# Where the narrow matmuls of a software-pipelined attention stand, and four distances of the stages behind it

## The chip, the cores and the metric

The program runs on one core of a Trainium2 chip. The metric is the device time of one execution in microseconds (us). The engines of the core are TensorE (PE, with its weight load PEld), VectorE (DVE), ScalarE (ACT), GpSimd (POOL) and SyncE (SP, which here only issues DMA transfers); each works through its own row of instructions in order and waits on semaphores.

## The reference

Three stages follow each other; the output of one is the input of the next.

```python
# 1: attention inside hash buckets: 2 batches, 8 heads, 768 positions, 64 dims, 6 hash bits
q_bits = (np.einsum('bhsd,dk->bhsk', q, proj) > 0)          # k_bits in the same way
mask = q_bucket[:, :, :, None] == k_bucket[:, :, None, :]
scores = np.where(mask, scale * np.matmul(q, k.transpose(0, 1, 3, 2)), -1000000000.0)
attn = np.exp(scores - np.max(scores, axis=-1, keepdims=True))
attn = attn / (np.sum(attn, axis=-1, keepdims=True) + 1e-09)
attn_out = np.matmul(attn, v)
# 2: mixture of experts on x = attn_out as (1536, 512): 8 experts, top 2, hidden width 1024
noisy_logits = x @ w_gate + np.log1p(np.exp(x @ w_noise)) * noise
out[mask] += top2_w[mask, k, None] * (np.maximum(x[mask] @ w1[e], 0.0) @ w2[e])   # each e, k
# 3: (1536, 512) -> 2048 -> 512
h = x @ w_in
return (h - np.tanh(h)) @ w_out
```

`w_in` and `w_out` come as 64-bit floats and are converted on the chip, in 16 blocks.

## The kernel before

**Attention.** An item is one batch and head; there are 16, and a pair of items (one group) shares the tiles of keys and queries. Time is laid out in *frames*. The table `plan` (filled by `at_frame`, from the offsets in `PLAN`) says which functions run in which frame; item `i` begins at frame 12 `i`. Every frame has one `smax` (a matmul of scores, L414, whose row maximum DVE takes in L415) and one `st_unit` (the transposed scores, two matmuls L448 and L449, then the exponential on ACT, L450). In every second frame comes a `pv` (the product with the values, L474, four matmuls of 64 output columns). Around these stand, once or a few times for each item or group: `prep_t` (three transposes of keys or queries, L271, then copies and remainders on ACT and DVE, L277, L284, L285), `prep_signs` (the hash bits, eight matmuls of 32 columns, L302), `mchain` and `mrows` (the maxima, put as extra rows into the queries, L434 and L438), `vmean` (L462), `psum` (partial sums of the exponentials on POOL or DVE, L483), `sums` (row sums, six matmuls of 32 columns, L490; a copy on ACT, L494, in the next frame; two transposes, L499, in the one after), `evac` (the output copied by ACT, transposed on PE some frames later, L523, scaled by DVE, L527, added up by POOL, L529). Once a pair of heads is done, `gate_t` transposes it for the router (L535) and `gate_wide` multiplies it with the router's weights (32 columns, L596).

**What sets the order.** `frame()` first takes one step of every generator left over from earlier frames and then calls the frame's tasks in the order in which `at_frame` got them. PE, DVE, ACT and SP keep the order in which the code is written; the row of POOL is ordered by the scheduler of the tile framework. Seven PSUM banks go round in rings: three for the tag `a` (turns, signs, sums, output transposes, maxima, router), two for `b` (smax), two for `c` (st_unit); `d`, the outputs, has one. `mchain` takes an `a` bank and keeps it until `mrows` and its DVE product L438 are done.

**The router and the experts.** When batch 0 is through, `gate(0)` runs its chain of small DVE operations in the frames behind `GF` (L624 to L707); its result `sidx` is the index list for `scatter(0)`, twelve indirect DMAs that POOL issues (L711). When batch 1 is through, `gate(1)` runs, and PE fills its steps with pieces of expert 0 (`seg_fine`, taken by `fill`; `FILL` has the number of pieces ahead of each step of the gate; a piece is half of a hidden block, six matmuls L1122, or one output block). Its matmuls for positions are L689 and L755. Segment 1 follows: hidden blocks (L1033 to L1035) and output blocks (L1058 to L1060) in steps numbered `f`; after a few of them all engines take a branch for overflow (L1219, L1220). `load_x(n + 1)` (L1013, L1016) loads the gathered tokens of the next segment and `trans_x` transposes them (L1026; copy on ACT L1027, remainder on DVE L1028). From step `(1, CV1)` on, `convert_more` converts blocks of the 64-bit weights (ACT L877, then DVE) and `fetch64` loads them (L866, L868). `store()` issues finished stores, `fetch()` loads the next expert weights (L840, L842), `next_w()` splits them (ACT L815, POOL L814).

Of the kernel before, what the change touches and what calls it, by code (L numbers as in the profile page):

```python
# [19 lines left out]
WB2 = 2  # L20
PF = 3

FILL = (1, 0, 3, 0, 3, 1, 0, 0, 2, 0, 0, 0)
FILL2 = 2
TX = (2, 2, 0, 0)
BANKS = {'a': [0, 1, 7], 'b': [2, 3], 'c': [4, 5], 'd': [6]}

PLAN = dict(turn=(-23, -15, -19, -10), turn1=(-20, -18, -13, -10), sign=(-12, -7), sign2=5, sign1=(-9, -7), gap=0,
            load=-37, load_v=-13, clear=-8, vsum=-1, vmean=15, gate_t=(58, 55), gate_wide=60, pv=3,
            psum=(5, 7, 8, 11, 14), nmterm=9, evac=13, evac_wait=10, sums=16, sums_wait=0, scatter=19, gate_w=25,  # L30
            pre_w=29, pre_b=-18, zero=26, trans=-12, open=-22, mrows=(13, 13), second=(-3, -2, -1, 0),
            init=(2, 4, 18), gates=(28, 31))

# [13 lines left out]

POOL1 = 7

CV1 = 4  # L50

CVN = 2

# [23 lines left out]
def body(tc, q, k, v, proj, w_gate, w_noise, noise, w1, w2, w_in, w_out, out):  # L77
    nc = tc.nc
    PS = bass.MemoryType.PSUM
    B, H, S, D = q.shape  # L80
# [19 lines left out]
    with ExitStack() as ctx:  # L100
# [792 lines left out]
        def convert_more(n):  # L893

            for _ in range(n):
                if hd.get("cv") is None and RAW64:
                    hd["cv"] = convert(*RAW64.pop(0))
                if hd.get("cv") is not None and next(hd["cv"], 1) is not None:
                    hd["cv"] = None
                    if RAW64:  # L900
                        hd["cv"] = convert(*RAW64.pop(0))
                        next(hd["cv"])
# [4 lines left out]
        def frame(tasks):  # L907

            going = list(running)
            running.clear()  # L910
            for gen in going:
                if next(gen, 1) is None:
                    running.append(gen)
            for f, *a_ in tasks:
                gen = f(*a_)
                if gen is not None and next(gen, 1) is None:
                    running.append(gen)
# [14 lines left out]
        def at_frame(t, f, *a_):  # L932
            plan.setdefault(t, []).append((f, *a_))
# [22 lines left out]
        for g in range(NI // 2):  # L956
            G = 24 * g
            for n, (w_, hf) in enumerate(KQ):
                if g:
                    at_frame(G + PLAN["turn" if g > 1 else "turn1"][n], prep_pool if g == 1 and POOL1 >> n & 1 else prep_t, g, w_, hf)  # L960
                    if w_ == "q":
                        at_frame(G + PLAN["sign" if g > 1 else "sign1"][hf], prep_signs, g, hf)
                else:
                    at_frame(PLAN["second"][n], prep_second, w_, hf)
            at_frame(max(G + PLAN["clear"], 0), clear_m, g)
            at_frame(G + PLAN["vsum"], vsum, g)
            at_frame(G + PLAN["vmean"], vmean, g)
            if g:
                at_frame(max(G + PLAN["load"], 0), load, g)
                at_frame(max(G + PLAN["load_v"], 0), load_v, g)  # L970
            b, P = divmod(g, NP)
            if g + 1 < NI // 2:
                at_frame(G + PLAN["gate_t"][0], gate_t, b, P, 0)
                at_frame(G + PLAN["gate_t"][1], gate_t, b, P, 1)
                if P % 2:
                    at_frame(G + PLAN["gate_wide"], gate_wide, b, (P - 1, P), P == KD4 - 1)
                elif b == B - 1 and P == KD4 - 2:
                    at_frame(G + PLAN["gate_wide"], gate_wide, b, (P,), True)
        GF = 24 * NP + LAG + 28
        at_frame(GF, gate, 0)  # L980
        for wh in range(2):
            at_frame(GF + PLAN["scatter"] + 3 * wh, scatter, 0, wh)
# [35 lines left out]
        def trans_x(n, dc):  # L1018
            e, b, r0, rows, nb = segs[n]
            m, tail = blocks(n)  # L1020
            if dc == 0:
                XH[n] = mx[n % 2].tile([128, KD4, CAP], F32R, name="xh")
                XL[n] = mx[n % 2].tile([128, KD4, CAP], F32R, name="xl")
            ps = bank("a")
            for j, m_ in enumerate([m] * nb + [128] * (tail > 0)):
                nc.tensor.transpose(ps[:, j * m:j * m + m_], xgs[n][0][:m_, j, ck(dc)], ident[:m_, :m_])  # L1026
            nc.scalar.activation(XH[n][:, dc, :rows], ps[:, :rows], AF.Copy)  # L1027
            nc.vector.tensor_tensor(XL[n][:, dc, :rows], ps[:, :rows], XH[n][:, dc, :rows].bitcast(F32), op=ALU.subtract)  # L1028
# [366 lines left out]
        for n in range(1, NSG):  # L1395
            last = n == NSG - 1
            if n == NSG - B:
                rings["C2"] = ctx.enter_context(tc.tile_pool(name="wC2", bufs=WC2, reuse_waits="tile"))
                store()
                mid.close()  # L1400
                del rings["st"]
                rings["C"] = ctx.enter_context(tc.tile_pool(name="wC", bufs=WC, side="right", reuse_waits="tile"))
            if last:
                store()
                m2 = ctx.enter_context(tc.tile_pool(name="m2", bufs=2, side="right", reuse_waits="tile"))
                gb2 = m2.tile([128, 1], F32, name="gb2")
                nc.vector.memset(gb2, G2 / (2 * G3))
                gsb = m2.tile([128, 1], F32, name="gsb")
                nc.vector.memset(gsb, -GS)
            fx = 2 if n == B - 1 else 1  # L1410
            for f in seg_steps(n, None if last else n + 1):
                if (n, f) == (1, IFS):
                    sched.close()
                    overflow()
                    manual()
                store()
                while fn[0] < min(wn[0] + (PF if "st" in rings else 1), len(wsrc)):
                    fetch()
                if not last and f == fx:
                    load_x(n + 1)  # L1420
                for dc in range(0 if last else KD4):
                    if f == (5 + dc // 2 if n == B - 1 else 3 + dc):
                        trans_x(n + 1, dc)
                if (1, CV1) <= (n, f) < (NSG - B, 0):
                    convert_more(CVN)
                    while conv64 and len(RAW64) + (hd.get("cv") is not None) < 2:
                        fetch64(conv64.pop(0))
                if segs[n][1] in (None, B - 1) and (f in LASTW if last else n >= B or f >= W1) or n == NSG - B and f in LASTV:
                    next_w()
                if B <= n < B + WN0 - NF and f == 4:  # L1430
                    next_w()
                for j in range(BC if last else 0):
                    if f == 1 + j // 2:
                        gather(j)
                    if f == 4 + j:
                        combine(j)
                        flush(1)
                    if f == 3 + j:
                        mix(j)
                        flush(1)  # L1440
# [51 lines left out]
```

## Time and profile before

| what | us |
|---|---|
| three timed executions | 941.16, 941.60, 941.63 (median 941.6) |
| the profiled execution's own time | 935.87 |
| span of the profiled execution, first to last instruction | 934.0 |
| PE busy in it | 898.5 (96%) |
| DVE, ACT, POOL busy | 673.6, 540.2, 366.9 |

The span is what the trace covers; the other 1.87 us of the profiled execution lie outside it. The mean clock granted to PE is 0.988 of full speed. Attention ends at about 299 us, expert 0 and the gate of batch 1 at about 334 us, and from about 375 us to the end PE is busy without a gap apart from a few near 660 to 690 us. A matmul's listed length overlaps with that of the next one, so the distance from start to start is its cost on PE.

### The profile page before, as it was taken

What the parts mean: (1) busy time and instruction counts of PE and PEld (TensorE: products, weight loads), DVE (VectorE), ACT (ScalarE), POOL (GpSimd) and SP (SyncE); (2) the same over time, 40 slices, a digit from 0 to 9 for tenths busy, and PEclk for the clock granted to TensorE, in tenths of its full rate; (3) what the DMA queues carried; (4) which work ended last, traced back from release to release, by engine and by line L of the source; (5) the groups of instructions that cost most, each with busy time, mean ns of one, the idle gap of its engine ahead of it and who ended that gap; (6) DMA issues with size and microseconds to landing.
All of it is one profiled execution on the core that took longest, in us unless ns stands there. A gap on an engine that the chain in (4) does not pass through costs nothing.

```text
span 934.0 us, 13624 instructions
## 1 busy us (share of the span) xinstructions
PE 898.5 (96%) x4736; PEld 700.0 (75%) x4736; DVE 673.6 (72%) x1289; ACT 540.2 (58%) x1039; POOL 366.9 (39%) x323
## 2 busy tenths in 40 slices
PE   8999999988899889999999999999999999999998
PEld 3555555544456777888888888888889899989997
DVE  7778777789655617787887878555888677677665
ACT  7658667655356234444444444354777777777765
POOL 6677778763875644000000004502342342342221
PEclk9999999999999998999999999999999999999999
DMA  5635543311401467786959586555420110110000
GB/s 122 176 100 172 168 155 106 114 40 42 156 12 46 168 203 233 274 291 200 314 185 342 188 271 219 169 174 179 134 69 1 57 46 1 57 46 1 35 1 34
DMA packets 104624, 123.72 MB, mean 132 GB/s; under 512 B 32120, under 2 KB 75176, under 8 KB 104552
## 3 DMA queue, kind: packets, MB, share of 16 engines
q1 hardware_dynamic: 100712, 110.23, 37.3%
q0 software_dynamic: 3840, 12.59, 4.0%
q8 instruction: 38, 0.62, 0.3%
q14 instruction: 34, 0.28, 0.1%
HBM read 82.79 MB, written 37.72 MB: 129 GB/s over the span
## 4 chain that ended last, share of the span: by engine, by line
PE 78%; DVE 10%; DMA 4%; POOL 2%; issue 2%; ACT 2%; SPq 1%; DVEq 0%; POOLq 0%; ACTq 0%
PE bank L1034 9%; PE bank L1035 9%; PE bank L1033 9%; PE bank L1060 9%; PE bank L1059 9%; PE bank L1058 8%; PE bank L474 6%; PE bank L448 4%; PE bank L449 3%; PE bank L414 3%; DMA Xg<-x,sidx 3%; PE bank L1075 2%; DVE mx L415 1%; PE bank L1026 1%; PE bank L302 1%
## 5 line engine op out<-in xcount | busy, mean ns | idle before, releaser
L1033 PE MATMUL bank<-xh,wt 128*128 128x384 f32 (+2 forms) x544 | 187.0, 344 | 5.5 <-DVE g_u L1346 2.7
L1034 PE MATMUL bank<-xl,wt 128*128 128x384 f32 (+2 forms) x544 | 183.7, 338 | 0.2 <-DVE xl L1028 0.2
L1035 PE MATMUL bank<-xh,wt 128*128 128x384 f32 (+2 forms) x544 | 183.7, 338 | 0.0
L814 POOL TENSOR_TENSOR wt<-wraw,wt 128x512 fp32r<-128x512 f32 x48 | 68.5, 1449 | 248.2 <-DVE cv_g L879 203.7
L1060 PE MATMUL bank<-wt,hh 128*128 128x512 f32 (+1 forms) x400 | 158.3, 396 | 0.4 <-DVE hh L1051 0.2
L1058 PE MATMUL bank<-wt,hh 128*128 128x512 f32 (+1 forms) x400 | 158.2, 396 | 0.3 <-ACT hh L1049 0.3
L1059 PE MATMUL bank<-wt,hh 128*128 128x512 f32 (+1 forms) x400 | 157.9, 395 | 0.0
L1337 POOL TENSOR_TENSOR g_th<-g_h,g_th 128x384 f32<-128x384 f32 x64 | 67.1, 1049 | 187.9 <-ACT g_th L1336 187.3
L450 ACT ACTIVATE p<-bank 128x384 f32<-128x384 f32 x192 | 92.0, 489 | 69.4 <-PE bank L449 61.3
L415 DVE TENSOR_REDUCE mx<-bank 128x1 f32<-128x384 f32 x192 | 103.1, 551 | 38.4 <-PE bank L414 36.3
L1033 PEld LDWEIGHTS bank<-xh,wt 128*128 128x128 f32 x544 | 103.0, 189 | 15.0 <-DVE g_u L1346 4.8
L1034 PEld LDWEIGHTS bank<-xl,wt 128*128 128x128 f32 x544 | 103.0, 189 | 7.1 <-DVE xl L1028 0.5
L1035 PEld LDWEIGHTS bank<-xh,wt 128*128 128x128 f32 x544 | 102.9, 189 | 3.0
L815 ACT ACTIVATE wt<-wraw 128x1024 fp32r<-128x1024 f32 x80 | 84.2, 1054 | 31.7 <-PE bank L1075 22.4
L1060 PEld LDWEIGHTS bank<-wt,hh 128*128 128x128 f32 (+1 forms) x400 | 74.9, 187 | 18.5 <-DVE hh L1051 0.8
L483 POOL TENSOR_TENSOR ps<-ps,p 128x768 f32<-128x768 f32 x45 | 82.1, 1825 | 10.7 <-ACT p L450 5.9
L1049 ACT ACTIVATE hh<-bank 128x448 fp32r<-128x448 f32 (+1 forms) x80 | 38.0, 475 | 81.0 <-PE bank L1035 40.2
L1058 PEld LDWEIGHTS bank<-wt,hh 128*128 128x128 f32 (+1 forms) x400 | 75.3, 188 | 12.7 <-ACT hh L1049 0.5
L474 PE MATMUL bank<-p,v 128*64 128x384 f32 x384 | 84.7, 520 | 0.0
L1059 PEld LDWEIGHTS bank<-wt,hh 128*128 128x128 f32 (+1 forms) x400 | 75.1, 188 | 12.8
L448 PE MATMUL bank<-qc,kb 108*128 108x384 f32 (+1 forms) x192 | 80.1, 417 | 2.6 <-DVE qc L438 2.5
L1051 DVE SCALAR_TENSOR_TENSOR hh<-bank,hh 128x384 fp32r<-128x384 f32 (+2 forms) x128 | 45.7, 388 | 42.9 <-ACT hh L1049 38.4
(250 smaller groups left out, 1625.5 us busy)
## 6 DMA issues: line engine op xcount, KB each, us to landing
wraw<-in_moe_w_dram SPq DMA_DIRECT2D x128, 256.0 KB
cv_t<-in_moe_w_in_dram SPq DMA_DIRECT2D x16, 512.0 KB
cv_t<-in_moe_w_out_dram SPq DMA_DIRECT2D x16, 512.0 KB
W2f<-cv_w SPq DMA_DIRECT2D x16, 512.0 KB
wraw<-W2f SPq DMA_DIRECT2D x16, 512.0 KB
Xg<-zero SPq DMA_DIRECT2D x14, 512.0 KB
Y<-zero SPq DMA_DIRECT2D x9, 512.0 KB
xy<-Xg SPq DMA_DIRECT2D x6, 768.0 KB
```

The costliest lines, as they stand in the source:

```text
L415: nc.vector.tensor_reduce(MX[i % 2][:, c, hf:hf + 1], ps[:, :HF], op=ALU.max, axis=AX.X)
L448: nc.tensor.matmul(ps[:, :HF], KB[sn(g, par)][r, ck(kc)], QC[sn(g, par)][r, half(hf)], start=True, stop=False)
L450: nc.scalar.activation(hd["p", i, kc][:, half(hf)], ps[:, :HF], AF.Exp, scale=float(D) ** -0.5)
L474: nc.tensor.matmul(hd["o", i][hf * D:(hf + 1) * D, :HF], raw["v", g][:, par, kc], hd["p", i, kc][:, half(hf)], start=(kc == 0), stop=(kc = ...
L483: eng.tensor_tensor(t, hd["p", i, 0] if kc == 1 else t, hd["p", i, kc], op=ALU.add)
L815: nc.scalar.activation(t[:, 0], r, AF.Copy)
L1033: nc.tensor.matmul(ps[:, :n], ws(0, dc), xh[:, dc, :n], start=(dc == 0), stop=False)
L1034: nc.tensor.matmul(ps[:, :n], ws(0, dc), xl[:, dc, :n], start=False, stop=False)
L1035: nc.tensor.matmul(ps[:, :n], ws(1, dc), xh[:, dc, :n], start=False, stop=(dc == KD4 - 1))
L1058: nc.tensor.matmul(ps[:m], a, t[:, 0, 1], start=first, stop=False)
L1059: nc.tensor.matmul(ps[:m], a, t[:, 1, 1], start=False, stop=False)
L1060: nc.tensor.matmul(ps[:m], l, t[:, 0, 1], start=False, stop=last)
```

## The change

It has six parts.

1. `frame()` sorts the frame's tasks: `pv` behind the others, then `sums`, `prep_signs` and `gate_wide`, and `evac` last.
2. Offsets in `PLAN`: `sums` 16 to 17 and `gate_wide` 60 to 64 (the last one, `gate_last`, stays at 60); `turn` and the signs at other frames, so that signs fall into frames that have a `pv`; `vmean` 15 to 17.
3. `evac_wait` 10 to 11: the output's transposes come one frame later behind their copy.
4. `GF` two frames later: `gate(0)` and the two halves of its scatter move with it.
5. `FILL[8]` 2 to 4: two more pieces of expert 0 ahead of gate(1)'s position matmuls.
6. In segment 1: conversion begins at step 7 instead of 4, its first load at step 3; segment 2's tokens are loaded at step 0 instead of 2.

```diff
-FILL = (1, 0, 3, 0, 3, 1, 0, 0, 2, 0, 0, 0)
+FILL = (1, 0, 3, 0, 3, 1, 0, 0, 4, 0, 0, 0)
...
-PLAN = dict(turn=(-23, -15, -19, -10), turn1=(-20, -18, -13, -10), sign=(-12, -7), sign2=5, sign1=(-9, -7), gap=0,
...
+PLAN = dict(turn=(-23, -17, -20, -14), turn1=(-20, -18, -13, -10), sign=(-12, -8), sign2=5, sign1=(-8, -6), gap=0,
...
-CV1 = 4
+CV1 = 3
...
-            for f, *a_ in tasks:
+
+            order = {pv: 1, sums: 2, prep_signs: 2, gate_wide: 2, evac: 3}
+            for f, *a_ in sorted(tasks, key=lambda t_: order.get(t_[0], 0)):
...
-                    at_frame(G + PLAN["gate_wide"], gate_wide, b, (P,), True)
-        GF = 24 * NP + LAG + 28
+                    at_frame(G + PLAN["gate_last"], gate_wide, b, (P,), True)
+        GF = 24 * NP + LAG + 30
...
-            fx = 2 if n == B - 1 else 1
+            fx = 0 if n == B - 1 else 1
...
+                if (1, CV1 + 4) <= (n, f) < (NSG - B, 0):
+                    convert_more(CVN)
                 if (1, CV1) <= (n, f) < (NSG - B, 0):
-                    convert_more(CVN)
```

PE around the sums of item 4 (L490), before. A name left of the arrow is the bank written, `p` and `v` are exponentials and values, `ss` the copied sums.

```order
L474 MATMUL bank_1381<-p,v_98 64x384 x2
L448 MATMUL bank_1389<-qc_168,kb_166 128x384
L449 MATMUL bank_1389<-ql_169,kl_167 128x384
L414 MATMUL bank_1393<-kb_158,qc_160 128x384
L490 MATMUL bank_1396<-ps,ones 32x256 x3
L535 MATMUL bank_1400<-ident,x 128x128 x3
L448 MATMUL bank_1407<-qc_168,kb_166 128x384
L449 MATMUL bank_1407<-ql_169,kl_167 128x384
L414 MATMUL bank_1411<-kb_158,qc_160 128x384
L474 MATMUL bank_1381<-p,v_98 64x384 x2
L499 MATMUL bank_1418<-ident,ss 128x96 x2
```
The same place after:

```order
L535 MATMUL bank_1396<-ident,x 128x128 x3
L271 MATMUL bank_1400<-ident,k 128x128 x3
L448 MATMUL bank_1408<-qc_168,kb_166 128x384
L449 MATMUL bank_1408<-ql_169,kl_167 128x384
L414 MATMUL bank_1412<-kb_158,qc_160 128x384
L474 MATMUL bank_1385<-p,v_98 64x384 x2
L490 MATMUL bank_1419<-ps,ones 32x256 x3
L448 MATMUL bank_1429<-qc_168,kb_166 128x384
L449 MATMUL bank_1429<-ql_169,kl_167 128x384
L414 MATMUL bank_1433<-kb_158,qc_160 128x384
L499 MATMUL bank_1436<-ident,ss 128x96 x2
```
The sums stood alone between wide matmuls and their transposes L499 behind a later value product; now the sums stand directly behind a value product, and L499 three wide matmuls behind them.

PE around the sums of item 12, before; L535 are the transposes for the router that need POOL's L529 of item 11:

```order
L474 MATMUL bank_2979<-p,v_96 64x384 x2
L448 MATMUL bank_2983<-qc_153,kb_151 128x384
L449 MATMUL bank_2983<-ql_154,kl_152 128x384
L414 MATMUL bank_2987<-kb_158,qc_160 128x384
L490 MATMUL bank_2990<-ps,ones 32x256 x3
L535 MATMUL bank_2994<-ident,x 128x128 x3
```
and after:

```order
L474 MATMUL bank_2976<-p,v_96 64x384 x2
L448 MATMUL bank_2983<-qc_153,kb_151 128x384
L449 MATMUL bank_2983<-ql_154,kl_152 128x384
L414 MATMUL bank_2987<-kb_158,qc_160 128x384
L535 MATMUL bank_2990<-ident,x 128x128 x3
L448 MATMUL bank_2995<-qc_153,kb_151 128x384
L449 MATMUL bank_2995<-ql_154,kl_152 128x384
L414 MATMUL bank_2999<-kb_158,qc_160 128x384
L474 MATMUL bank_2976<-p,v_96 64x384 x2
L490 MATMUL bank_3006<-ps,ones 32x256 x3
```
The transposes L535 keep their frame and the sums come one frame behind them, where before they stood ahead.

SP at the load of segment 2's tokens, before, behind the branch:

```order
L842 DMA wraw<-in_moe_w_dram 128x512
L840 DMA wraw<-in_moe_w_dram 128x4x128
L842 DMA wraw<-in_moe_w_dram 128x512
L1013 DMA xy<-Xg 128x1536
L1016 DMA xy<-Xg 128x512
```
and after, ahead of the branch (L1015 and L1018 are L1013 and L1016 of before):

```order
L842 DMA wraw<-in_moe_w_dram 128x512
L1015 DMA xy<-Xg 128x1536
L1018 DMA xy<-Xg 128x512
L840 DMA wraw<-in_moe_w_dram 128x4x128
L842 DMA wraw<-in_moe_w_dram 128x512
L1222 COMPARE_AND_BRANCH
```
The load moved ahead of the branch and of two pairs of weight loads.

## Rows read from the trace of the kernel before

**Rows 1.** Windows: width, PE, PEld, DVE, ACT, POOL busy (instructions), clock, DMA, GB/s.
```profile
75.00:100.00 25.00, 25.00 (x149) 13.96 (x146) 19.79 (x42) 18.00 (x39) 20.34 (x19) 1.00 0.39 118
100.00:125.00 25.00, 23.43 (x142) 13.66 (x140) 18.56 (x40) 18.31 (x38) 19.15 (x17) 1.00 0.45 138
200.00:225.00 25.00, 21.18 (x113) 11.81 (x114) 24.14 (x73) 14.11 (x32) 7.73 (x10) 0.93 0.00 1
375.00:650.00 275.00, 275.00 (x1408) 240.00 (x1408) 203.76 (x292) 123.27 (x176) 30.70 (x22) 1.00 0.71 236
```

**Rows 2.** Waits of PE to 375 us: waiter, releaser: total, times, longest.
```profile
PE bank L414 <- DVE mx L415: 6.2, 5, 1.9
PE bank L523 <- DVE qc L438: 3.1, 2, 1.6
...
PE bank L689 <- DVE M L675: 2.5, 1, 2.5
...
PE bank L1026 <- DMA xy<-Xg: 2.0, 1, 2.0
PE bank L1033 <- ACT xh L1027: 1.5, 1, 1.5
```

**Rows 3.** Timeline of PE: start, length, line, shape, count [idle before <-releaser].
```profile
84.98 0.87 PE L474 MATMUL bank<-p,v 128*64 128x384 f32 x4
85.78 0.52 PE L302 MATMUL bank<-kl,pj 128*32 128x384 f32 x2
...
91.83 0.34 PE L449 MATMUL bank<-ql,kl 128*128 128x384 f32 x1
92.00 0.33 PE L414 MATMUL bank<-kb,qc 128*128 128x384 f32 x1
92.27 0.52 PE L302 MATMUL bank<-kl,pj 128*32 128x384 f32 x2
...
93.05 0.44 PE L448 MATMUL bank<-qc,kb 108*128 108x384 f32 x1
93.33 0.34 PE L449 MATMUL bank<-ql,kl 128*128 128x384 f32 x1
```

**Rows 4.** Timeline of PE around the sums of item 2.
```profile
78.55 0.63 PE L490 MATMUL bank<-ps,ones 128*32 128x256 f32 x6
79.11 0.55 PE L535 MATMUL bank<-ident,x 128*128 128x128 f32 x3
```

**Rows 5.** Timeline of PE, the sums of item 4.
```profile
109.59 0.63 PE L490 MATMUL bank<-ps,ones 128*32 128x256 f32 x6
```

**Rows 6.** Line L494 (ACT): its engine sat idle until.
```profile
  PE bank L490: 6.1, 8
```

**Rows 7.** Timeline of ACT, the same sums of item 2.
```profile
79.90 0.37 ACT L494 ACTIVATE ss<-bank 96x256 f32<-96x256 f32 x1
```

**Rows 8.** Timeline of DVE, the gate of batch 0.
```profile
194.60 1.70 DVE L631 TENSOR_SCALAR g_ln<-g_u 128x48 f32<-128x48 int32 x1
...
226.65 0.17 DVE L707 CAST sidx<-g_p 128x12 int32<-128x12 f32 x1
```

**Rows 9.** Timeline of POOL, first scatter and the step behind it.
```profile
227.13 1.19 POOL L711 DMA_INDIRECT Xg<-x,sidx  x1 [8.12 <-DVE sidx L707]
...
251.19 0.99 POOL L529 TENSOR_TENSOR x<-x,xt 128x384 f32<-128x384 f32 x1
```

**Rows 10.** Timeline of PE, the sums of item 12.
```profile
253.05 1.07 PE L490 MATMUL bank<-ps,ones 128*32 128x256 f32 x6 [2.74 <-DVE ps L483]
```

**Rows 11.** Timeline of PE, two fine pieces of expert 0.
```profile
301.54 0.27 PE L1122 MATMUL bank<-xh,wt 128*128 128x240 f32 x1
...
302.88 0.40 PE L1058 MATMUL bank<-wt,hh 128*120 128x512 f32 x1
```

**Rows 12.** Window behind gate(1)'s position matmuls, at the lower clock.
```profile
307.80:311.00 3.20, 3.20 (x30) 3.20 (x27) 2.30 (x13) 0.00 (x0) 1.07 (x2) 0.50 0.02 5
```

**Rows 13.** Timeline of ACT, the first conversion.
```profile
354.49 1.12 ACT L877 ACTIVATE cv_g<-cv_t 128x1024 f32<-128x1024 f32 x1 [4.16 <-DMA cv_t<-in_moe_w_out_dram]
```

More of the change, by code (lines that the diff above doesn't have):

```diff
@@ L26 @@
 BANKS = {'a': [0, 1, 7], 'b': [2, 3], 'c': [4, 5], 'd': [6]}
-PLAN = dict(turn=(-23, -15, -19, -10), turn1=(-20, -18, -13, -10), sign=(-12, -7), sign2=5, sign1=(-9, -7), gap=0,
-            load=-37, load_v=-13, clear=-8, vsum=-1, vmean=15, gate_t=(58, 55), gate_wide=60, pv=3,
-            psum=(5, 7, 8, 11, 14), nmterm=9, evac=13, evac_wait=10, sums=16, sums_wait=0, scatter=19, gate_w=25,
+PLAN = dict(turn=(-23, -17, -20, -14), turn1=(-20, -18, -13, -10), sign=(-12, -8), sign2=5, sign1=(-8, -6), gap=0,
+            load=-37, load_v=-13, clear=-8, vsum=-1, vmean=17, gate_t=(58, 55), gate_wide=64, gate_last=60, pv=3,
+            psum=(5, 7, 8, 11, 14), nmterm=9, evac=13, evac_wait=11, sums=17, sums_wait=0, scatter=19, gate_w=25,
             pre_w=29, pre_b=-18, zero=26, trans=-12, open=-22, mrows=(13, 13), second=(-3, -2, -1, 0),
```

## The prediction

> **What bounds the kernel now.** I read the table of busy time by stage first. In the windows of 25 us PE is busy throughout in four of the ten between 50 and 300 us (75:100 is one of them), in two more it lacks at most one wait (100:125 lacks 1.57 us), and in the other four it lacks 2 to 4 us, as in 200:225, where DVE is busy 24.14 of 25 us; from 375 us on PE is full [rows 1]. So nothing that the change does behind 375 us can give much, time in attention is worth its full price in about six windows of ten, and in the others DVE or a wait has the last word. The list of PE's waits comes next: before 375 us it names few, each with its releaser [rows 2]. Last, the timeline of PE, for the price of a narrow matmul between wide ones, and those of DVE, POOL and ACT around a few waits.
>
> **Narrow matmuls behind the value product.** Two wide matmuls follow each other at 0.17 us (91.83 to 92.00). From a wide one to the first sign (L302) it is 0.27 (92.00 to 92.27), and from the wide one behind the signs to the next 0.28 (93.05 to 93.33): 0.10 on the way in and 0.11 on the way out, about 0.2 for a group that stands alone. The signs behind L474 begin 0.80 after it started (84.98 to 85.78), which is what four matmuls of the value product take anyway, so the way in costs nothing there, and the way out is paid once for both [rows 3]. In PE's row of the program the groups that come directly behind a wide matmul fall from 21 to 3: 18 by 0.19 is 3.4 us, of which six windows of ten keep 2.0 (bounds 0 and 3.4). **Term: -2.0.** The Trainium skill, TensorEngine Tiling (Array Packing), section Key Properties, states that changing the tiling mode drains the TensorE. By it the step from 64 to 32 columns would be a change too, and a group moved would save one change of three, 1.0 in place of 2.0, and the sum below would be 1.0 less; the row from L474 to L302 shows no such price, so the row decides.
>
> The trade has a cost side. Transposes stand directly ahead of a value product 14 times now and never before; no row shows that pair. Nearest is a wide matmul's 0.10 into a narrow mode, so between 0 and 14 by 0.10; a gain has no reason. I take half. **Term: +0.7.**
>
> **The transposes of the sums.** Before, a value product lies between L490 and L499, and L499 waits for nothing. Now three wide matmuls do. In item 2, L490 starts at 78.55 and takes 0.56 [rows 4], ACT's copy L494 ends at 79.90 + 0.37 = 80.27, which is 1.72 behind the start [rows 7]; PE will be back at 0.56 + 0.10 + 3 by 0.175 = 1.19, and wait 0.53. ACT sat idle ahead of L494 in 8 of the 16 items [rows 6], and there the copy is in time; in the other 8 it was behind other work, as here. 8 by 0.53 by six tenths is 2.5. Bounds: 0 (the sums move a frame, so ACT may have another job in hand) and 16 by 0.53 = 8.5. **Term: +2.5.**
>
> **The output's transposes.** L523 waits twice, 3.1 us in all, for L438, the product of `mrows`, which frees the bank that `mchain` held [rows 2]. One frame later another bank of the ring is next. What is late next is PE itself: around both waits it is full. Bounds 0 and -3.1, and I take the whole. **Term: -3.1.**
>
> **The router of batch 0.** Between the sums of items 2 and 4 lie 24 frames and 31.04 us [rows 4, 5], 1.29 a frame. Its list is ready at 226.65 [rows 8] and POOL issues the first scatter at 227.13, having been idle for 8.12 us; L529 of item 11 ends at 251.19 + 0.99 = 252.18 [rows 9]. In POOL's row eleven scatter DMAs, one L529, one L510 and four partial sums stand between, before as after, so the whole of it comes 2.6 us later. PE came to this frame at 253.05 - 2.74 = 250.31 and waited with the sums until 253.05 [rows 10]. Now L535, which needs L529, stands there first: 252.18 + 2.6 = 254.8, a wait of 4.5 in place of 2.74. Behind it on PE lie all scores of item 13, and DVE and ACT, which live off them. Bounds 0 (if the list comes no later) and +2.6. **Term: +1.7.**
>
> **Expert 0 and segment 1.** Twelve matmuls L1122, two pieces, take 302.88 - 301.54 = 1.34 [rows 11]; they go into the wait of L689 for M, 2.5 us, and shorten it as much [rows 2]. **Term: -1.3** (bounds 0, where segment 1's tokens are then late, and -1.3). Segment 2's tokens are waited for 2.0 at L1026 [rows 2]; issued ahead of the branch, two pairs of weight loads earlier, they are there in time. **Term: -2.0** (bounds 0 and -2.0). SP's row pays: the weights behind this load are issued later by two issues, and the load itself waits for the last scatter of batch 1. The first conversion stood on ACT 4.16 us for its load [rows 13], and L1033 waited 1.5 behind it [rows 2]. That goes, but the 64-bit loads now stand ahead of a weight load of segment 1, whose split on ACT will wait; one for the other, 0, with bounds -1.5 and +2.0. The weights' conversion ends later in its own stage, where PE is full [rows 1], and costs nothing; without that cover it would cost its three steps.
>
> **The clock.** Behind the wait of L689 PE runs at the lower of its two levels, 1.2 GHz (granted clock 0.50), for 3.2 us [rows 12], which loses 1.6. There are two such stretches; the other, not shown, is behind the wait for segment 2's tokens. The waits of 1.57 at L523 left the clock at 1.00 [rows 1]. L689's wait falls to 1.2 and the other goes, but new waits come: I count one of the two. **Term: -1.6** (bounds -3.2 and +1.6).
>
> The other edits (`vmean`, `evac` last in its frame, turns at other frames) move work on engines with room; the nearest row are the five waits for DVE's maxima, 1.2 each [rows 2], so +-1.2.
>
> **Sum:** -2.0 + 0.7 - 3.1 + 2.5 + 1.7 - 1.3 - 2.0 - 1.6 = -5.1. The profiled execution took 935.87 us (span 934.0 and 1.87 around it) and would take 930.8. The median of the timed runs is 5.7 above the profiled one; I keep that distance: 941.6 - 5.1 = 936.5.
>
> **Rivals.**
> - *No new waits.* ACT's copy is in time, L535 finds L529 ready, transposes ahead of value products are free, all 18 groups count, the conversion's wait goes, and both low-clock stretches go: -5.1 - 2.5 - 1.7 - 0.7 - 1.4 - 1.5 - 1.6 = -14.5, **927.1**. Against it: POOL had no slack between first scatter and L529, and half of the copies were late already.
> - *What is won is given back at the next wait.* In attention the five terms make -2.0 + 0.7 - 3.1 + 2.5 + 1.7 = -0.2; if segment 1 only trades its wait for tokens against one for weights, and the clock falls as often, that is all: **941.4**. For it: SP issues everything of that stretch in one row.
> - *The router's chain on DVE gets slower.* Two frames later, the small operations of `gate(0)` meet other POOL work. L631 took 1.70 us there; L707, of the same chain, took 0.17 [rows 8]: 1.5 lost in one operation while POOL was at work. DVE is the bound in that stretch [rows 1], so PE pays each. Four more of the kind eat the 5.1; with six more it is 9.0 - 5.1 = +3.9: **945.5**. For it: the later the chain, the more of POOL's sums and scatters stand beside it. Against it: POOL was busy for only 7.73 of the 25 us from 200 on [rows 1]. The Trainium skill, SBUF — State Buffer, section SBUF: two separate sides, has VectorE and GpSimd share one pair of ports as an exclusive lock for a whole instruction; the 1.70 agrees.
>
> **How the numbers follow.** Forecast 0.40, no new waits 0.12, given back 0.20, slower chain 0.28. About 0.2% (1.9 us) is what a measurement of this kernel can tell from no change: faster 0.40 + 0.12 = 0.52, same 0.20, slower 0.28. The forecast's own range is 933 to 939. The wide range holds it, the second rival and most of the third, and no more than the edge of the first: 930 to 946.
>
> **What would show it.** In the profile after: signs and sums at 0.80 behind the start of L474, no 1.57 at L523; L499 with waits of about 0.5 for ACT in half of the items; L535 waiting 4 to 5 us for L529 near 250 us; L689's wait near 1.2; no wait for tokens at segment 2. The forecast is wrong if attention ends more than 2 us later or earlier than it did, or if L1026 still waits.

## The result, and the profile after

The change made the kernel slower. Four runs of each on one chip: before 941.62 us (median), after 951.75 us, a ratio of 1.0102 with a 95% interval of 1.0075 to 1.0129. Forecast were 936.5 us and a range of 930 to 946.

The profiled execution of after took 951.35 us with a span of 949.6, near its median. That of before was 5.7 us below its median, as the prediction said, so the spans (949.6 against 934.0) differ by 15.6 us where the timed runs differ by 10.1. A standstill of 7.2 us, told below, is in the trace of after and not in that of before.

Two windows of before that [rows 1] does not show, and then the windows of after, in the columns of [rows 1]: width, then busy time of PE, PEld, DVE, ACT, POOL with instruction counts, granted clock, DMA share, GB/s.

```profile
50.00:75.00 25.00, 25.00 (x133) 13.85 (x135) 18.77 (x42) 14.69 (x30) 18.30 (x17) 0.93 0.49 148
250.00:275.00 25.00, 22.26 (x120) 12.46 (x118) 14.04 (x31) 10.69 (x23) 18.00 (x13) 0.93 0.20 57
```

```profile
50.00:75.00 25.00, 21.36 (x113) 11.63 (x112) 18.53 (x43) 12.51 (x26) 16.17 (x15) 0.93 0.39 116
200.00:225.00 25.00, 20.52 (x98) 10.96 (x97) 23.10 (x65) 13.00 (x31) 11.33 (x11) 0.86 0.07 20
250.00:275.00 25.00, 19.98 (x95) 11.57 (x96) 17.45 (x35) 8.88 (x19) 20.44 (x15) 0.86 0.38 124
375.00:650.00 275.00, 271.99 (x1351) 236.64 (x1351) 211.28 (x299) 122.99 (x171) 32.96 (x20) 0.99 0.71 233
```

PE was full in 50:75 before and has 21.36 of 25 us now; in 200:225 and 250:275 it lost work and clock (0.86 where it was 0.93). From 375 us on it is nearly full, as in [rows 1], so most of the loss lies ahead of that.

The waits of PE in after up to 400 us, in the columns of [rows 2]:

```profile
PE bank L414 <- DVE mx L415: 8.3, 5, 3.0
PE bank L1060 <- issue: 7.2, 1, 7.2
PE bank L434 <- DVE nm L428: 6.2, 3, 5.0
PE bank L499 <- ACT ss L494: 3.2, 6, 1.2
PE bank L1060 <- DVE wraw L1092: 3.0, 1, 3.0
...
PE bank L689 <- DVE M L675: 1.2, 1, 1.2
```

L689 fell from 2.5 to 1.2, and L523, not shown, from 3.1 to 1.1, as planned; L1026's line (L1028 in after) is gone from the list. In their place stand 8.3 for DVE's maxima (6.2 before), 6.2 at L434, 3.2 at L499, and two waits in the experts, 7.2 and 3.0. The wait of 7.2 us at 337.81 has "issue" as its releaser, that is nothing that the trace names; PE, DVE and ACT stand still together. The traces of e5 to e8 below show the same standstill, also ahead of an output block of expert 0: 4.32 us at 327.40, 3.42 at 330.23, 4.16 at 331.61 and 4.55 at 326.02. In e8:

```profile
PE bank L1059 <- issue: 4.5, 1, 4.5
```

These four were timed on a chip on which the kernel before took 941.2 us, and after on one with 941.6; no trace from a chip on which it took 934 to 936 us has the standstill. None of the four has the change's parts 5 and 6, so these do not make it. It is left out of the account, and its cause stays open.

For where the time goes I use one mark for all runs: the start of the sums L490 of an item, one row for each item in PE's timeline, like those in [rows 4] and [rows 5]. The stretches between the sums of items 1 and 8 hold the seven items in which PE is the bound; those from 8 to 12 hold the router of batch 0. In the runs with the sums at offset 17 the sums of items 0 to 14 stand one frame (1.3 us) later and those of the last item do not.

| run | start of item 0 | 0 to 1 | 1 to 8 | 8 to 12 | 12 to 15 |
|---|---|---|---|---|---|
| before | 41.46 | 22.79 | 109.83 | 78.97 | 41.14 |
| after | 44.79 | 25.33 | 113.24 | 84.03 | 38.04 |
| attention part (e2) | 43.99 | 26.12 | 113.24 | 83.56 | 38.07 |
| order only (e5) | 43.03 | 22.85 | 112.41 | 80.22 | 39.43 |
| turns and signs only (e6) | 41.08 | 25.75 | 112.10 | 80.37 | 42.28 |
| attention, old turns (e7) | 44.63 | 24.96 | 108.31 | 86.22 | 38.03 |
| router two frames later only (e9) | 41.95 | 22.78 | 109.78 | 89.17 | 39.62 |
| output's transposes of two items (e11) | 42.01 | 21.29 | 108.32 | 81.39 | 42.13 |
| the same, and signs (e12) | 41.34 | 25.99 | 109.38 | 79.49 | 39.61 |
| attention, router back (e14) | 43.73 | 24.98 | 113.11 | 78.64 | 38.15 |
| attention, both back (e15) | 43.82 | 24.06 | 109.08 | 77.88 | 39.05 |
| router two frames earlier (e13) | 41.33 | 21.29 | 109.82 | 77.09 | 39.60 |
| router three frames earlier (e18) | 41.62 | 22.79 | 109.78 | 74.78 | 39.61 |

After is behind before by 3.3 (of which a frame is 1.3), 2.5, 3.4 and 5.1, and takes 3.1 back at the end (1.3 of it the frame): 11.2 us at the sums of the last item. The stretch from 0 to 1 is noisy: the second trace of before has 21.29 there (last section).

### The profile page after: what moved, and what is told of

The parts are those of the page before. It is cut to its first block, busy times and chain, and to the rows that moved or that the text cites. A ratio compares the mean times of both kernels' runs of the same rounds, so it can differ in the third digit from the quotient of the medians.

```text
span 949.6 us, 13628 instructions
## 1 busy us (share of the span) xinstructions
PE 902.7 (95%) x4736; PEld 703.0 (74%) x4736; DVE 677.7 (71%) x1289; ACT 540.9 (57%) x1039; POOL 369.7 (39%) x323
## 4 chain that ended last, share of the span: by engine, by line
PE 55%; DVE 2%; ACT 1%; issue 1%; POOL 0%; DVEq 0%; POOLq 0%
PE bank L1035 9%; PE bank L1037 9%; PE bank L1036 9%; PE bank L1062 8%; PE bank L1061 8%; PE bank L1060 8%; PE bank L1077 2%; PE bank L1028 1%; DVE g_u L1346 1%; PE bank L1315 1%; DVE wt L814 0%; DVE hh L1364 0%; DVE g_u L1348 0%; DVE g_u L1358 0%; ACT hh L1359 0%
## 5 line engine op out<-in xcount | busy, mean ns | idle before, releaser
L483 POOL TENSOR_TENSOR ps<-ps,p 128x768 f32<-128x768 f32 x45 | 82.1, 1825 | 10.1 <-ACT p L450 5.4
L474 PE MATMUL bank<-p,v 128*64 128x384 f32 x384 | 85.9, 527 | 0.0
L448 PE MATMUL bank<-qc,kb 108*128 108x384 f32 (+1 forms) x192 | 80.0, 417 | 1.7 <-DVE qc L438 0.9
```

Of the source, the lines that this page charges most:

```text
L448: nc.tensor.matmul(ps[:, :HF], KB[sn(g, par)][r, ck(kc)], QC[sn(g, par)][r, half(hf)], start=True, stop=False)
L474: nc.tensor.matmul(hd["o", i][hf * D:(hf + 1) * D, :HF], raw["v", g][:, par, kc], hd["p", i, kc][:, half(hf)], start=(kc == 0), stop=(kc = ...
L483: eng.tensor_tensor(t, hd["p", i, 0] if kc == 1 else t, hd["p", i, kc], op=ALU.add)
```

## Experiments

All ratios are to the kernel before on the same chip, with their 95% interval. The runs were made on several chips: the kernel before took 934 to 936 us on most of them and 941.2 us on that of e5 to e8.

### Whose profile: the kernel before again (e1)

No edit.

> The kernel before, once more, for a second trace of it. Its first profiled execution took 935.87 us where its timed runs took 941.16 to 945.09. Theory A (the profiled execution was a lucky one and a typical one holds a stall that the first trace lacks): about 941 us, with one idle stretch of 4 to 8 us on TensorE near expert 0 that has no counterpart in the first trace, as the changed kernel shows one of 7.21 us at 337.81. Theory B (the difference is spread out): about 941 us with every wait a little longer, and none above 3 us that the first trace does not show.

It took 935.59 us with a span of 933.8, and the kernel before ran at a median of 935.18 beside it. On this chip the level itself was 6 us lower, so the run could not decide between the theories: it has no stall and no lengthened waits, and no trace of the kernel before was taken at 941 us. The traces of e5 to e8, which were, have the stall that theory A asks for. That it makes the difference between the levels is likely by this, and not shown. The first profile of before is that of an ordinary execution at the lower level.

### Attention against the rest (e2, e3)

e2 has the parts 1 to 4 of the change, e3 the parts 5 and 6.

```diff
 # e2: after, with
-FILL = (1, 0, 3, 0, 3, 1, 0, 0, 4, 0, 0, 0)
+FILL = (1, 0, 3, 0, 3, 1, 0, 0, 2, 0, 0, 0)
-CV1 = 3
+CV1 = 4
-            fx = 0 if n == B - 1 else 1
+            fx = 2 if n == B - 1 else 1
...
-                if (1, CV1 + 4) <= (n, f) < (NSG - B, 0):
+                if (1, CV1) <= (n, f) < (NSG - B, 0):
                     convert_more(CVN)
-                if (1, CV1) <= (n, f) < (NSG - B, 0):
 # e3: before, with the opposite
```

> All of the change inside attention (order within the frames, the PLAN offsets, evac_wait, the router two frames later), with FILL, CV1 and the load of segment 2's tokens as before. Theory 1 (the loss is made in attention: transposes ahead of value products, waits of L499 for ACT, the start and the router of batch 0): 8 to 13 us slower than before. Theory 2 (the loss is made behind attention, in expert 0 and segment 1): within 3 us of before.

> Only what the change does behind attention: two more pieces of expert 0 ahead of gate(1)'s positions, conversion from step 7, segment 2's tokens at step 0. Theory 1 (the loss is made in attention): 2 to 5 us faster than before. Theory 2 (the loss is made behind attention): 5 to 11 us slower.

e2: 1.0111 (1.0086 to 1.0136), as much as the whole change. e3: 1.0002 (0.9982 to 1.0021). The loss is made in attention; but what I forecast behind it did not come either. PE's waits of e3 between 300 and 420 us:

```profile
PE bank L1026 <- DMA xy<-Xg: 3.5, 1, 3.5
PE bank L1058 <- DVE wraw L1090: 3.4, 1, 3.4
PE bank L1033 <- ACTq L1220: 2.3, 1, 2.3
PE bank L689 <- DVE M L675: 1.2, 1, 1.2
```

L689 waits 1.2 in place of 2.5, and segment 2's tokens no longer make PE wait. But PE now reaches segment 1's tokens early and waits 3.5 at 322.66, where before it waited for none, 3.4 for an output copy of DVE (L1090) that stands behind the split weights, and 2.3 at the branch in place of 1.3. Listed waits come to 10.6 us; before they were 8.0 in the same stretch. The second rival, "given back at the next wait", held here.

### The output's transposes (e4, e11)

```diff
 # e4
-            ... evac=13, evac_wait=10,
+            ... evac=13, evac_wait=11,
 # e11: one frame later for the two items that waited
-                at_frame(J + LAG + PLAN["evac"], evac, i)
+                at_frame(J + LAG + PLAN["evac"], evac, i, 11 if i in (4, 8) else PLAN["evac_wait"])
```

> Only evac_wait 11 in place of 10, which takes the output's transposes out of the frame in which their bank is held. If the two waits of 1.57 us at L523 are worth their length: 3 us faster. If the transposes meet the next value product instead and pay for that, 16 times 0.1 to 0.2 us: 0 to 1 us faster. If another step of the items becomes late: slower.

> The kernel before with the output's transposes one frame later for items 4 and 8 alone, the two that waited 1.57 us. If such a wait is worth its length and the run with evac_wait 11 lost it again through the other items: 2 to 3.5 us faster. If what is gained there is lost at the router's stretch, which DVE and POOL pace: within 1 us of before.

e4: 0.9994 (0.9978 to 1.0010). e11: 1.0008 (0.9990 to 1.0026). In e11 the stretch from 1 to 8 is 108.32 in place of 109.83, about the one wait of 1.57 that lies in it; the stretch from 8 to 12 is 81.39 in place of 78.97. There the other wait of 1.57 came back as another:

```profile
186.68 0.51 PE L462 MATMUL bank<-vs,ones 128*128 128x128 f32 x2 [2.25 <-DVE ql L285]
```

This is a wait of 2.25 at L462 for DVE's L285, which reads a bank of that ring. From about 187 to 190 us, behind it, the granted clock is at its lower level, which loses 1.7 us; behind the wait of 1.57 it had stayed at 1.00. So of two equal waits in one list one was worth 1.5 us in its stretch and the other lost more than it had cost, and the times of e4 and e11 show no gain at all.

### Order and turns (e5 to e8)

e5 has the sorted frames and all old offsets, e6 the new offsets of turns and signs in the old order, e7 is e2 with the old turns (the signs stay at their new frames), e8 is e5 with the sums at 17.

```diff
 # e5, e8
+            order = {pv: 1, sums: 2, prep_signs: 2, gate_wide: 2, evac: 3}
+            for f, *a_ in sorted(tasks, key=lambda t_: order.get(t_[0], 0)):
 # e6; e7 takes back the first of these, turn, in e2
-PLAN = dict(turn=(-23, -15, -19, -10), ... sign=(-12, -7), ... sign1=(-9, -7),
+PLAN = dict(turn=(-23, -17, -20, -14), ... sign=(-12, -8), ... sign1=(-8, -6),
```

> Only the order within the frames, no offset changed: transposes now stand ahead of value products (15 times, before never) and of what follows a value product only a few groups move. Theory X (the offsets of the turns make the loss): within 2 us of before. Theory Y (the order makes it, through transposes ahead of value products and the sums' transposes L499): 2 to 5 us slower.

> Only the offsets of the turns of keys and queries and of the signs, in the old order. Theory X (their copies on ACT and remainders on DVE fall where exponentials and maxima are queued): 4 to 9 us slower. Theory Y (the order makes the loss): within 2 us of before, or faster.

> The attention part of the change (the run before it of that part was 1.1% slower) with the offsets of the turns taken back, signs left at their new frames. Theory X: at least half of the 10 to 11 us is gone, 0 to 5 us slower than before. Theory Y: 8 to 11 us slower than before.

> The order within the frames and the sums one frame later, directly behind a value product; all other offsets old. By the prediction's terms for these alone: about 1.5 less for the sums' own switches (half of 2.0 and some), 0.7 more for transposes ahead of value products, 2.5 more for L499: 1 to 2 us slower. Theory X: within 2 us. Theory Y: 4 to 8 us slower.

e5: 1.0048 (1.0018 to 1.0078). e6: 1.0087 (1.0065 to 1.0109). e7: 1.0082 (1.0061 to 1.0102). e8: 1.0045 (1.0029 to 1.0062). Neither theory alone: turns and signs cost 8 us by themselves, the order 4, and without the turns the attention part still loses 8. e6 moves turns and signs together, so the table has to part them. From 1 to 8, e6 loses 2.3, and with the old turns (e7) the attention part is *faster* than before there (108.31): that loss is mostly the turns' (e14 and e15 below differ by 4.0). What e7 loses lies in the stretch of the router. Between 0 and 1 the loss is not the turns' alone: every run with the new sign frames takes 24.06 us or more there, with new turns (e2, e6, e14) and with old ones (e7, e12, e15), and every run with the old sign frames 22.87 or less. The order alone (e5) loses 2.6 from 1 to 8; e7 and e15, which have it too, do not, so other offsets take that back; which of them, no run shows.

What the turns do where PE is the bound is seen in after around the sums of item 4, the item of [rows 5]:

```profile
115.61 0.49 PE L271 MATMUL bank<-ident,k 128*128 128x128 f32 x3
116.14 0.44 PE L448 MATMUL bank<-qc,kb 128*128 128x384 f32 x1
116.42 0.34 PE L449 MATMUL bank<-ql,kl 128*128 128x384 f32 x1
116.85 0.44 PE L414 MATMUL bank<-kb,qc 96*128 96x384 f32 x1
117.22 0.87 PE L474 MATMUL bank<-p,v 128*64 128x384 f32 x4
118.02 0.63 PE L490 MATMUL bank<-ps,ones 128*32 128x256 f32 x6
...
119.04 0.34 PE L414 MATMUL bank<-kb,qc 96*128 96x384 f32 x1
119.80 0.38 PE L499 MATMUL bank<-ident,ss 96*128 96x96 f32 x2 [0.42 <-ACT ss L494]
```

```profile
118.30 0.48 ACT L277 ACTIVATE kb<-bank 64x384 fp32r<-64x384 f32 x1
118.82 0.52 ACT L284 ACTIVATE kl<-kb 64x384 fp32r<-64x384 f32 x1
119.37 0.38 ACT L494 ACTIVATE ss<-bank 96x256 f32<-96x256 f32 x1
```

The value product 117.22 and the sums 118.02 stand as planned, 0.80 apart. But L271 to L448 takes 0.53 where it took 0.25, and L449 to L414 takes 0.43 where two wide matmuls take 0.17: short waits of some 0.25 us, which no line of the list of waits names. Each of the two comes four times between 60 and 190 us. And L499 waits 0.42, because the copies of the keys' turn (L277, L284) are on ACT ahead of L494. With the old turns (e7) the same sums find ACT free:

```profile
116.02 0.38 ACT L494 ACTIVATE ss<-bank 96x256 f32<-96x256 f32 x1 [0.17 <-PE bank L490]
```

```profile
115.33 0.63 PE L490 MATMUL bank<-ps,ones 128*32 128x256 f32 x6
...
116.86 0.33 PE L499 MATMUL bank<-ident,ss 96*128 96x96 f32 x2
```

L494 begins 0.69 behind the start of L490, and L499 waits for nothing. In e7 no wait of PE is listed between 60 and 190 us.

### The router (e9, e10)

```diff
 # e9: before, with
-        GF = 24 * NP + LAG + 28
+        GF = 24 * NP + LAG + 30
 # e10: after, with
-            ... gate_w=25,
+            ... gate_w=37,
```

> Only the router of batch 0 and its scatter two frames later, all else as before. Theory R (the stretch of the router loses because its operations on DVE and POOL's scatter then stand beside POOL's sums): 2 to 6 us slower, with the loss between the sums of items 8 and 12. Theory X (the offsets of the turns make the loss there too): within 2 us of before.

> The whole change, with the router's weights of batch 0 (the small operations L727 to L745 on DVE) 12 frames later, where POOL's scatter and its sums of item 12 are through. In the changed kernel two of these, L740 and L745, took 2.40 and 2.56 us beside POOL's sums and PE waited 5.02 us at L434. Theory R: that wait is gone, 3 to 6 us faster than the changed kernel, so 4 to 8 us slower than before. If POOL's scatter itself holds the item and the small operations only fill its time: another wait of 3 to 5 us in its place (L535 for L529) and no gain.

e9: 1.0083 (1.0060 to 1.0105), 7.8 us for two frames. e10: 1.0171 (1.0142 to 1.0200), slower than after. The three engines in e9, DVE, POOL and PE:

```profile
242.75 2.15 DVE L727 TENSOR_TENSOR g_d<-g_v 128x6 f32<-128x6 f32 x1
...
248.43 2.46 DVE L740 TENSOR_TENSOR g_t<-g_ws,g_f 128x12 f32<-128x12 f32 x1
```

```profile
233.16 1.19 POOL L711 DMA_INDIRECT Xg<-x,sidx  x1 [14.79 <-DVE sidx L707]
...
246.03 1.83 POOL L483 TENSOR_TENSOR ps<-ps,p 128x768 f32<-128x768 f32 x1
248.03 0.99 POOL L711 DMA_INDIRECT Xg<-x,sidx  x1 [0.17 <-issue]
249.05 1.81 POOL L483 TENSOR_TENSOR ps<-ps,p 128x768 f32<-128x768 f32 x1
```

```profile
248.56 0.44 PE L414 MATMUL bank<-kb,qc 96*128 96x384 f32 x1 [2.37 <-DVE mx L415]
254.94 0.27 PE L434 MATMUL bank<-ident,n 128*12 128x128 f32 x1 [5.93 <-DVE nm L428]
```

Before, eleven scatter DMAs went out with one partial sum among them, the other three behind them, and L740 took 0.13 us:

```profile
240.55 0.13 DVE L740 TENSOR_TENSOR g_t<-g_ws,g_f 128x12 f32<-128x12 f32 x1
```

```profile
242.55 1.86 POOL L483 TENSOR_TENSOR ps<-p 128x768 f32<-128x768 f32 x1
244.58 0.99 POOL L711 DMA_INDIRECT Xg<-x,sidx  x1 [0.17 <-issue]
245.60 5.63 POOL L483 TENSOR_TENSOR ps<-ps,p 128x768 f32<-128x768 f32 x3
```

In e9 POOL's row alternates between a scatter DMA and a partial sum of 1.8 us, and four of DVE's small operations, L727 and L740 among them, take 2.15 to 2.56 us: they begin while POOL works and end when one of its sums does (248.43 + 2.46 = 250.89, and the sum 249.05 + 1.81 = 250.86). PE waits 2.37 and 5.93 behind them. It is the sums that hold them: in e18 below, with scatter DMAs alone beside them, L727 at 234.06 and L745 at 236.62 take 0.16 and 0.17. The Trainium skill, SBUF — State Buffer, section SBUF: two separate sides, describes the pair of ports that the two engines lock for a whole instruction, on VectorE's side for an operation with two inputs in SBUF among others; the two ends, 0.03 us apart, agree with it. Why L740 is held from 248.43 on, when POOL is still in a scatter DMA, no row shows. After has the same in L740 and L745:

```profile
250.18 2.40 DVE L740 TENSOR_TENSOR g_t<-g_ws,g_f 128x12 f32<-128x12 f32 x1
...
253.01 2.56 DVE L745 TENSOR_TENSOR wAB<-g_f 128x6 f32<-128x6 f32 x1
```

```profile
256.53 0.28 PE L434 MATMUL bank<-ident,n 128*12 128x128 f32 x1 [5.02 <-DVE nm L428]
```

e10 moved these operations away. The wait of 5.02 went, and this came:

```profile
264.95 0.90 PE L535 MATMUL bank<-ident,x 128*128 128x128 f32 x3 [6.46 <-POOL x L529]
...
277.66 0.69 PE L414 MATMUL bank<-kb,qc 128*128 128x384 f32 x1 [2.56 <-DVE mx L415]
```

```profile
239.99 1.19 POOL L711 DMA_INDIRECT Xg<-x,sidx  x1 [12.76 <-DVE sidx L707]
...
263.88 1.02 POOL L529 TENSOR_TENSOR x<-x,xt 128x384 f32<-128x384 f32 x1
```

That is the wait of L535 for L529 which the prediction had put at 4.5 us; in after it had been covered by the other. POOL needs 24.9 us from its first scatter to the end of L529, as before (25.05), and starts too late. At their new place the moved operations met POOL's next sums, and PE waited 2.56 behind them; the lower clock took 6.9 us more than in after (20.5 against 13.6, counted as in the clock's item below). I expected 3 to 6 us of gain; the alternative written beside it, another wait in its place, is what came.

### Both taken back (e14, e15), signs alone (e12)

```diff
 # e14: e2, with
-            ... gate_wide=64,
+            ... gate_wide=62,
-        GF = 24 * NP + LAG + 30
+        GF = 24 * NP + LAG + 28
 # e15: e14, with turn=(-23, -15, -19, -10)
 # e12: e11, with sign=(-12, -8), sign1=(-8, -6), and
+            order = {smax: 0, st_unit: 0, pv: 0, sums: 1, prep_signs: 1, gate_wide: 1}
+            for f, *a_ in sorted(tasks, key=lambda t_: order.get(t_[0], 2)):
```

> The attention part of the change with the router at its old frame (GF 28; the wide products of the router at offset 62 instead of 64, so that its sums are there). If the router's place and the turns are two separate causes: 3 to 6 us slower than before, the start and the stretch between the sums of items 1 and 8 unchanged against the attention part, and the stretch from 8 to 12 shorter by 3 to 6. If the turns alone make the stretch from 8 to 12 long too: 8 to 12 us slower.

> The attention part with both the router's frame and the turns' offsets taken back: what is left is the order in the frames, sums and signs and wide products behind value products, and the output's transposes one frame later. If the two are the whole loss: within 3 us of before, with 108 to 109 us between the sums of items 1 and 8 (before 109.8) and 79 to 82 between 8 and 12. If the order itself loses at the start and at the router: 4 to 8 us slower.

> As the run with items 4 and 8, and the signs at the change's new frames and directly behind a value product, with all transposes behind that as before and the turns and sums at their old frames. If the switch saved is worth 0.19 us for a group: 4 groups fewer alone and 5 more behind a value product, 1 us faster than the run without; if not, the same as it. Any loss of over 2 us against it would say that the signs' own frames matter.

e14: 1.0059 (1.0042 to 1.0075). e15: 1.0012 (1.0001 to 1.0022). e12: 1.0024 (1.0010 to 1.0037). With the router back the stretch from 8 to 12 falls from 83.56 to 78.64, and those from 1 to 8 and from 12 to 15 stay; with the turns back too, 1 to 8 falls from 113.11 to 109.08, and all but a tenth of a per cent of the loss is gone. So taking these two back takes the loss away: 4.9 us for the router (e2 to e14, by the ratios) and 5.2 for the turns (e14 to e15, on one chip). The parts do not add up, though: alone they cost 7.8 (router), 8.2 (turns and signs) and 4.5 (order), 20.5 us, and together 10. e12 lost 1.6 us against e11 in these times, and its stretch from 0 to 1 is 25.99 against 21.29. In its trace a second small DVE operation of the start stands beside a partial sum and takes 1.73 us at 49.60 (L575, 0.17 before), ending at 51.33 with a sum that ends at 51.32, and the wait of L414 behind it is 3.66 where it was 1.62. That is the pattern of e9 again; no run takes it away.

### The router earlier (e13, e16, e18), and with the new order (e17)

```diff
 # e13, e16, e18: before, with
-        GF = 24 * NP + LAG + 28
+        GF = 24 * NP + LAG + 26      # e16: 27, e18: 25
 # e17: e15, with gate_wide=60 and GF = 24 * NP + LAG + 26
```

> The kernel before with the router of batch 0 and its scatter two frames earlier instead of later. If the loss of 8 us for two frames later is a slope (POOL's scatter comes ahead of its sums the more, the earlier it starts): 2 to 5 us faster. If it is a step (only which of DVE's small operations meet POOL's sums counts, and before none does): within 2 us of before.

> The kernel before with the router one frame earlier. Slope: 1 to 3 us faster. Step: within 2 us of before.

> The kernel before with the router three frames earlier. If the slope goes on: 4 to 5 us faster. If at two frames the scatter is already out of the way: 2 to 4 us faster, as there. If the router now waits for the last head's logits: slower than two frames earlier.

> The attention part with old turns (the run with both taken back: 0.1% slower than before) and the router two frames earlier (alone: 0.3% faster than before). If they add up: 2 to 3 us faster than before. If the earlier router's gain needs the old order (its small operations between POOL's jobs): within 1 us of before, or slower.

e16: 0.9985 (0.9975 to 0.9996). e13: 0.9966 (0.9952 to 0.9980). e18: **0.9950 (0.9931 to 0.9969)**, 4.3 us faster than the kernel before by the medians, and better than both kernels. e17: 1.0022 (1.0006 to 1.0038): the two do not add up. Ratios at 25, 26, 27, 28 and 30 are 0.9950, 0.9966, 0.9985, 1 and 1.0083: a slope, steeper on the late side. POOL in e18:

```profile
221.30 1.19 POOL L711 DMA_INDIRECT Xg<-x,sidx  x1 [3.49 <-DVE rec L504]
...
236.58 0.97 POOL L711 DMA_INDIRECT Xg<-x,sidx  x1 [0.30 <-issue]
237.56 1.04 POOL L529 TENSOR_TENSOR x<-x,xt 128x384 f32<-128x384 f32 x1
...
239.47 1.84 POOL L483 TENSOR_TENSOR ps<-p 128x768 f32<-128x768 f32 x1
...
246.98 1.01 POOL L529 TENSOR_TENSOR x<-x,xt 128x384 f32<-128x384 f32 x1
```

All twelve scatter DMAs are out ahead of the first partial sum of item 12, and L529 ends at 247.99, ahead of the frame that needs it. The wait of 2.74 at its sums [rows 10] is gone from e18, and the lower clock behind it too. The same three microseconds of the two kernels, in the order before, e18:

```profile
253.00:256.00 3.00, 2.95 (x14) 1.71 (x16) 0.97 (x3) 1.24 (x3) 2.40 (x2) 0.51 0.31 98
```

```profile
253.00:256.00 3.00, 3.00 (x21) 1.62 (x21) 1.92 (x7) 1.53 (x4) 2.69 (x3) 1.00 0.00 0
```

What the granted clock lacks to 1, summed over windows of 1 us from 20 to 420 us, is 10.2 us before and 3.4 in e18. That is this one execution, with a mean clock of 0.996. The other five of e18 had 0.988 to 0.991, as the kernel before had beside them (0.987 to 0.991), and took 927.5 to 932.2 us against 933.2 to 937.2. So the gain does not rest on the clock.

## Why the prediction was wrong

The sign was wrong, and the sums of the last item stood 11.2 us later where the prediction allowed 2 for the end of attention. Step by step, with the stretch from 1 to 8 as the place where PE is the bound:

- **The router** (term +1.7). This is the step that failed first. The mechanism was there, two frames late against a POOL row without slack, and the wait of L535 for L529 came to 6.46 in e10 where 4.5 was said; in after another wait stood ahead of it. But the term priced that wait alone. The same delay also brought partial sums of 1.8 us between the scatter DMAs, and DVE's small operations beside them. The order of POOL's row showed that alternation; I used it only to count that both rows hold the same jobs. By itself the delay measured +7.8, in the whole 4.9. My third rival, the slower chain on DVE, named the mechanism, at 0.28, with a price of 1.5 for an operation; in e9 they took 2.15 to 2.56.
- **Turns and signs** ("work on engines with room", bounds 1.2 either way; the signs' new frames had no cost in any term). This is the other step that failed. The two alone measured +8.2, the turns in the whole 5.2; what the signs' frames cost by themselves is open but for the 1.6 of e12. ACT is busy some 72% of the time in such windows [rows 1], but in the frame of L494 it was not free: a share of busy time says nothing on one frame. The term for L499 (+2.5) was near in size (3.2 listed), but not for its reason, three wide matmuls being too short for ACT's copy: four of its waits, 0.42 and 0.43, lie between 60 and 190 us, and with the same matmuls and the old turns there is none.
- **Narrow matmuls** (-2.0) and transposes ahead of value products (+0.7). The prices held: 0.80 from L474 to the sums; and 0.42 from L271 to L474 where L271 to L448 takes 0.25, which is 0.07 more than the 0.10 that a wide matmul ahead of L474 paid. What they bring together is small: 1 to 8 is 108.31 in e7 and 108.21 in e4, which has neither, so nothing was left of a forecast 1.3. No run has these two terms alone.
- **The output's transposes** (-3.1). Half of it in the stretch where PE is the bound, 1.5; the other wait was replaced by one of 2.25, and the time did not change (e4, e11). "What is late next is PE itself" was wrong for the second of the two.
- **Expert 0 and segment 1** (-1.3 and -2.0), **the clock** (-1.6). The waits of L689 and of segment 2's tokens went as said and others of the same size came; e3 measured no difference. On the clock the sign was wrong for the whole, since the term let the new waits keep one low stretch of two, and more came than that. In windows of 1 us from 20 to 420 us, the sum of what the granted clock lacks to 1 is 10.2 us before and in e1 and 8.5 in e3, but 13.6 in after, 3.4 more than before, and 15.4 in e9. The 1.7 that e3 lacks are no gain of its edit: they lie at 51 to 56 us, where e1 has none either, and behind 300 us both before and e3 lose 5.1. Nor are there two such stretches behind 300 us in the trace of before, as the prediction read, but three: 307 to 312, 348 to 353, 358 to 363.

The rivals do not fall one by one: what came is the third for the router, the second for segment 1, and a cause that no rival had, the turns.

## What to carry to other kernels

A step that is moved by whole frames takes its neighbours on every engine with it: set out the row of each shared engine for the frame where it lands, and not the count of its jobs. Ahead of a wait that a slow queue ends, the place of that queue's start is worth more than the order of the waiting engine: three frames earlier gave 4.3 us here, two frames later cost 7.8, while of all the switches saved on PE no gain could be measured. Of two equal waits in a list, ask for each what the same bank or engine does in the frame to which the work goes.

## What the runs showed that I had not expected

- The stretch between the sums of items 0 and 1 took 22.79 us in one trace of the kernel before and 21.29 in the other, with the same waits; the difference is the granted clock from 52 to 56 us, 0.61 in the first and 1.00 in the second:

```profile
52.00:56.00 4.00, 4.00 (x18) 1.72 (x17) 2.10 (x8) 0.98 (x2) 3.75 (x6) 0.61 0.00 0
```

```profile
52.00:56.00 4.00, 4.00 (x26) 1.62 (x24) 3.80 (x10) 2.10 (x4) 3.76 (x6) 1.00 0.00 0
```

- In after PE lost 2.1 us between 60 and 190 us by eight waits of 0.25 to 0.28 us which no list of waits names; they show only as distances from start to start, such as 0.43 for L449 to L414.
- A standstill of 3.4 to 7.2 us near expert 0 is in all five traces of kernels timed where the kernel before took 941 us, and in none of the others. Nothing in the traces says what releases it.
